# Attention decode: the last head's output is written from its 128x4 tile by one DMA of 2-byte elements

## The chip, the core and the metric

The kernel runs on one core of a Trainium2 chip. The metric is the device time of one execution in microseconds (us). Before the change the median of three runs is 628.26 us (628.16 to 628.30).

## What is computed

One decode step of grouped-query attention. There are 32 query heads with one query each, and 8 key/value heads of 65,536 positions, each of 128 numbers in bf16. Four query heads share one key/value head.

```python
B, Hq, Hkv, Sq, Sk, D = 1, 32, 8, 1, 65536, 128

def reference(q, k, v):
    rep = Hq // Hkv                       # 4 query heads to a key/value head
    k = jnp.repeat(k, rep, axis=1)
    v = jnp.repeat(v, rep, axis=1)
    scale = D ** -0.5
    scores = jnp.einsum("bhqd,bhkd->bhqk", q, k) * scale
    p = softmax(scores, axis=-1)
    return jnp.einsum("bhqk,bhkd->bhqd", p, v)
```

The result is 32 rows of 128 bf16 numbers, 8 KB in all, one row after the other in DRAM. The keys and values read for it are 268 MB.

## The kernel before

Each key/value head is cut into four units of 16,384 positions, and two units make a pair: 16 pairs in all. For a unit TensorE transposes 128 blocks of 128 keys (`pe_transposes`, L135), VectorE and ScalarE copy the transposed blocks out of PSUM (`evict`, L207 and L205), TensorE multiplies them by the four queries of the head (`pe_scores`, L144), VectorE and GpSimd find the maximum, ScalarE takes the exponentials (`exps`), and TensorE sums the values weighted by them (`pe_values`, L162) into a PSUM tile `pvb` of 128 numbers by 4 queries. A running maximum and a running sum (`acc`, `lp`) join the units of a head.

Each engine has a queue of its own, written out by hand in `tensor_engine`, `vector_engine`, `scalar_engine`, `gpsimd_engine` and `sync_engine`, and waits on semaphores. SyncE (SP) issues all loads of keys and values in the order of use, and after them the stores.

The division by the softmax sum leaves a head's output in four columns of the SBUF tile `oT`, 128 numbers (partitions) by 4 queries: L310 for the heads before the last, L305 for the last one. In DRAM the 128 numbers of a query lie in a row, so the tile has to be turned round on its way there. The two cases differ:

- **Heads 0 to 6.** The columns are shifted along as heads come in, and in the last head's first half VectorE transposes all of `oT` in 32x32 blocks into `orow` (L282). SP writes `orow` by four DMAs of 28 rows of 64 bytes (L445), which are issued right behind the last loads.
- **Head 7, the last.** L305 writes the last four columns of `oT` and raises the semaphore `t_f`. TensorE, which waits for `t_f`, transposes the 128x4 columns into a PSUM tile `trb` of 4x128 (L191) and raises `s_x`. VectorE, which waits for `s_x`, copies this to the SBUF tile `lrow` of 4x128 (L339) and raises `t_row`. SP, which waits for `t_row`, writes `lrow` by one DMA of four rows of 256 bytes (L448), with the semaphore `l_sem`.

At the end of the block the engines meet at a barrier (the instructions at L450), and SP waits until all stores have landed: at L457 for `o_sem` (the four DMAs) and then for `l_sem`.

The semaphore `t_f` is raised once per head and never lowered, so that its value is 8 once the last head's output stands in `oT`.

Of the kernel before, what the change touches and what calls it, by code (L numbers as in the profile page):

```python
# [5 lines left out]
DT = mybir.dt  # L6
# [4 lines left out]
P = 128  # L11
# [30 lines left out]
def starts(sizes):  # L42
    return [sum(sizes[:i]) for i in range(len(sizes))]
# [8 lines left out]
def bass_standalone__gqa_softmax__decode_kernel(nc, q, k, v, out):  # L52
    _, Hq, _, D = q.shape
    _, H, Sk, _ = k.shape
    R = Hq // H
    HR = H * R
# [4 lines left out]
    kf, vf, qf, of = k[0], v[0], q[0, :, 0, :], out[0, :, 0, :]  # L61
# [4 lines left out]
    def sb(name, shape, dt):  # L66
        return S(nc.sbuf_tensor(name, shape, dt))

    def sem(name):
        return S(nc.semaphore(name))  # L70
# [10 lines left out]
    ident = sb("ident", [P, P], DT.bfloat16)  # L81
# [15 lines left out]
    oT = sb("oT", [P, HR], DT.bfloat16)  # L97
    otmp = sb("otmp", [P, HR], DT.bfloat16)
    orow = sb("orow", [P, HR], DT.bfloat16)
    lrow = sb("lrow", [R, D], DT.bfloat16)  # L100
    dscr = sb("dscr", [P, 2], DT.float32)

    trb = [S(nc.psum_tensor(f"trb{i}", [P, TB * P], DT.bfloat16)) for i in range(NTB)]
# [12 lines left out]
    cm, cma, ng, dmr, exd, sx, lrd, lra = (sem(n) for n in ("cm", "cma", "ng", "dmr", "exd", "sx", "lrd", "lra"))  # L116
    acr, l_sem, lws = sem("acr"), sem("l_sem"), sem("lws")
    xd, xa, xg = sem("xd"), sem("xa"), sem("xg")
    q_sem, o_sem, s_x, t_if, t_id, t_o, t_f, t_row = (
        sem(n) for n in ("q_sem", "o_sem", "s_x", "t_if", "t_id", "t_o", "t_f", "t_row"))  # L120

    def own(e, ins, s):
        ins.then_inc(s, 1)
        take(e, s)
# [43 lines left out]
    def pe_pair(pe, lap):  # L168
        pend = []
        for n in range(2):  # L170
            for j in range(G):
                pe_transposes(pe, n, j)
                pend.append((n, j))
                if len(pend) > LAG:
                    pe_scores(pe, *pend.pop(0))
        while pend:
            pe_scores(pe, *pend.pop(0))
        for n in range(2):
            pe_values(pe, n, lap)

    def tensor_engine(pe):
        pe.wait_ge(t_id, 1)
        for _ in range(PE_LEAD):
            pe.matmul(pvb[0][0:R, 0:R], lhsT=ident[:, 0:R], rhs=ident[:, 0:R], start=True, stop=True)
        pe.wait_ge(q_sem, 16)
        pe.transpose(qps[:, 0:HR], qsb[:, :], ident[0:HR, 0:HR]).then_inc(s_x, 1)
        pe.wait_ge(t_if, 1)
        with pe.Fori(0, NP) as lap:
            pe_pair(pe, lap)
        pe.wait_ge(t_f, H)  # L190
        pe.transpose(trb[0][0:R, 0:P], oT[:, HR - R:HR], ident[:, :]).then_inc(s_x, 1)  # L191


    def evict(e, n, j):
# [24 lines left out]
    def next_queries(e):  # L219
        e.tensor_copy(qcur[:, :], qT[:, 0:R]).then_inc(qrdy, 1)  # L220
        own(e, e.tensor_copy(qtmp[:, 0:HR - R], qT[:, R:HR]), xd)
        own(e, e.tensor_copy(qT[:, 0:HR - R], qtmp[:, 0:HR - R]), xd)
# [39 lines left out]
    def dve_pair(e, second, lap):  # L262

        fresh, last = not second, second
        for j in range(G):
            if not on_act(j):
                evict(e, 0, j)
            if j == 0:
                e.sem_inc(pgo, 1)
        for j in (0, 1, 2):  # L270
            evict(e, 1, j)
        take(e, qkd)
        chunk_max(e, 0)
        evict(e, 1, 4)
        new_max(e, 0, fresh)
        for j in (5, 6, 8, 9, 10):
            evict(e, 1, j)
        rescale(e, 0, fresh)
        if fresh:
            own(e, e.tensor_copy(otmp[:, 0:HR - R], oT[:, R:HR]), xd)  # L280
            own(e, e.tensor_copy(oT[:, 0:HR - R], otmp[:, 0:HR - R]), xd)
            e.transpose(orow[:, :], oT[:, :]).then_inc(t_o, 1)  # L282
        for j in (12, 13, 14):
            evict(e, 1, j)
        take(e, qkd)
        chunk_max(e, 1)
        new_max(e, 1, False)
        if last:
            next_queries(e)
        else:  # L290
            e.sem_inc(qrdy, 1)
        values_done(e, 0, fresh)
        rescale(e, 1, False)
        if not last:
            e.wait_ge(pvd, 1)
            e.sem_inc(vfree, 1)
            values_done(e, 1, False)
            return
        e.sem_inc(acr, 1)
        e.sem_inc(lrd, 1)  # L300
        take(e, lra)
        own(e, e.reciprocal(recip[:, :], la[:, :]), xd)
        with e.If(lap == H - 1):
            e.wait_ge(pvd, 1)
            e.tensor_tensor(oT[:, HR - R:HR], pvb[1][:, 0:R], recip[:, :], ALU.mult).then_inc(t_f, 1)  # L305
        with e.Else():
            e.wait_ge(pvd, 1)
            e.sem_inc(vfree, 1)
            own(e, e.tensor_tensor(acc[:, :], acc[:, :], pvb[1][:, 0:R], ALU.add), xd)
            e.tensor_tensor(oT[:, HR - R:HR], acc[:, :], recip[:, :], ALU.mult).then_inc(t_f, 1)  # L310
        e.sem_inc(pvd, -1)

    def make_identity(e):

        e.memset(ident[:, :], 0.0)
        for i in range(3):
            e.memset(ramp[:, i:i + 1], float(i))
        own(e, e.memset(ramp[:, 3:4], 3.0), xd)
        w = 4
        while w < Q:  # L320
            own(e, e.tensor_scalar(ramp[:, w:2 * w], ramp[:, 0:w], float(w), None, ALU.add), xd)
            w *= 2
        own(e, e.transpose(rampT[:, :], ramp[:, :]), xd)
        for b in range(0, P, Q):
            ins = e.tensor_tensor(ident[b:b + Q, b:b + Q], ramp[b:b + Q, :], rampT[b:b + Q, :], ALU.is_equal)
        ins.then_inc(t_id, 1)

    def vector_engine(e):
        make_identity(e)
        e.memset(oT[:, :], 0.0)  # L330
        e.memset(dm[:, :], 0.0)
        e.wait_ge(s_x, 1)
        own(e, e.tensor_copy(qT[:, :], qps[:, 0:HR]), xd)
        next_queries(e)
        with e.Fori(0, H) as lap:
            dve_pair(e, False, lap)
            dve_pair(e, True, lap)
        e.wait_ge(s_x, 2)
        e.tensor_copy(lrow[:, :], trb[0][0:R, 0:P]).then_inc(t_row, 1)  # L339


    def exps(e, n):
# [55 lines left out]
    def sync_engine(e):  # L398
        W = T * D

        def src(x, p):
            h, c = p // 2, p % 2
            return x[h, c * 2 * P * T:(c + 1) * 2 * P * T, :].rearrange("(p t) d -> p (t d)", p=P)

        def pieces(to, s, sizes, sems):
            for a, w, sm in zip(starts(sizes), sizes, sems):
                e.dma_start(to[:, a * D:(a + w) * D], s[:, a * D:(a + w) * D]).then_inc(sm, 16)

        def tokens(sems):
            for sm in sems:  # L410
                e.sem_inc(sm, 16)

        for p in range(NP):
            ks, vs = src(kf, p), src(vf, p)
            if p:
                e.wait_ge(kfree, 3 * p)
            if WHOLE[0] <= p < WHOLE[1]:
                e.dma_start(kbuf[:, :], ks).then_inc(kp[0][0], 16)
                tokens(kp[0][1:])
            else:  # L420
                for n in range(2):
                    if n and p:
                        e.wait_ge(bfree, p)
                    to, s = bbuf if n else kbuf, ks[:, n * W:(n + 1) * W]
                    if p == 0 or (p == NP - 1 and n == 0):
                        pieces(to, s, K_PIECES[n], kp[n])
                    else:
                        e.dma_start(to[:, 0:W], s).then_inc(kp[n][0], 16)
                        tokens(kp[n][1:])
                e.sem_inc(cpg, len(POOL_COPIES))  # L430
                e.sem_inc(cpa, len(sum(ACT_COPIES.values(), ())))
            if p:
                e.wait_ge(vfree, p)
            if WHOLE[0] <= p < WHOLE[1]:
                tokens(kp[1])
            if p < NP - 1:
                e.dma_start(vbuf[:, :], vs).then_inc(vp[0][0], 16)
                tokens(vp[1])
            else:
                for n in range(2):  # L440
                    pieces(vbuf[:, n * W:(n + 1) * W], vs[:, n * W:(n + 1) * W], V_PIECES[n], vp[n])
        e.wait_ge(t_o, H)
        for b, rows in enumerate(OUT_ROWS):
            for r, n in zip(starts(rows), rows):
                e.dma_start(of[r:r + n, b * Q:(b + 1) * Q],  # L445
                            orow[b * Q + r:b * Q + r + n, :]).then_inc(o_sem, 16)
        e.wait_ge(t_row, 1)
        e.dma_start(of[HR - R:HR, :], lrow[:, :]).then_inc(l_sem, 16)  # L448

    with nc.Block() as block:  # L450
        block.tensor(tensor_engine)
# [34 lines left out]
```

## Time and profile before

The profile is one execution, taken by the hardware profiler.

| What | us |
|---|---|
| Median of three runs | 628.26 |
| Span of the profiled execution, first to last instruction | 626.94 |
| What the median has beyond the span | 1.32 |
| Last weighted sum of values ends, L305 starts | 625.00 |
| TensorE's transpose L191 starts | 625.22 |
| VectorE's copy L339 starts | 625.52 |
| SP issues the last DMA, L448 | 625.77 |
| SP's last wait, L457, is over | 626.9 |

The profiled execution's own device time is not listed apart from its span; the 1.32 us are the median less the span.

How to read the rows. PE is TensorE, PEld its weight loads, DVE VectorE, ACT ScalarE, POOL GpSimd, SP SyncE; a q behind the name (SPq) marks instructions of an engine's sequencer, among them the issue of a DMA. L305 is line 305 of the program. A row of the timeline has the start, the duration in us, the engine, the line, the operation, output and input tile, their shapes, the number of instructions, and in brackets how long the engine had been idle and what ended that. A row on waits reads: who waited, for whom, us in total, times, longest. A view of DMA in a window divides the window into 40 slices: first the busy share of the 16 DMA engines in tenths, then the rate in GB/s, then the number of packets. A packet is one contiguous piece that one DMA engine moves, or the 4 bytes by which it raises a semaphore.

### The profile page before, as it was taken

What the parts mean: (1) busy time and instruction counts of PE and PEld (TensorE: products, weight loads), DVE (VectorE), ACT (ScalarE), POOL (GpSimd) and SP (SyncE); (2) the same over time, 40 slices, a digit from 0 to 9 for tenths busy, and PEclk for the clock granted to TensorE, in tenths of its full rate; (3) what the DMA queues carried; (4) which work ended last, traced back from release to release, by engine and by line L of the source; (5) the groups of instructions that cost most, each with busy time, mean ns of one, the idle gap of its engine ahead of it and who ended that gap; (6) DMA issues with size and microseconds to landing.
All of it is one profiled execution on the core that took longest, in us unless ns stands there. A gap on an engine that the chain in (4) does not pass through costs nothing. (4 is left out here: it accounts for less than half of the span.)

```text
span 626.9 us, 27931 instructions
## 1 busy us (share of the span) xinstructions
PE 484.6 (77%) x12340; PEld 478.9 (76%) x12340; DVE 315.1 (50%) x699; ACT 228.9 (37%) x445; POOL 159.9 (26%) x124
## 2 busy tenths in 40 slices
PE   5752995959859498694976959679496894999698
PEld 5752995949859498694976959679496894999698
DVE  4620752817537174371734717356183562848274
ACT  2320532615335153341634407245062441624133
POOL 0000704307042070520605115060150702400000
PEclk9965875958769587695966959678596785969597
DMA  8999999999999999999999999999999999999997
GB/s 366 440 449 424 439 431 439 431 439 426 443 422 447 410 460 410 460 406 460 410 439 431 426 443 426 443 426 439 431 439 431 439 431 435 416 447 424 420 433 302
DMA packets 6280, 268.57 MB, mean 428 GB/s; under 512 B 896, under 2 KB 1024, under 8 KB 1152
## 3 DMA queue, kind: packets, MB, share of 16 engines
q1 hardware_dynamic: 6224, 268.45, 99.2%
q8 instruction: 6, 0.10, 0.1%
q10 hardware_dynamic: 48, 0.01, 0.0%
q14 instruction: 2, 0.02, 0.0%
HBM read 268.44 MB, written 0.01 MB: 428 GB/s over the span
## 5 line engine op out<-in xcount | busy, mean ns | idle before, releaser
L207 DVE COPY ktb<-trb 128x1024 bf16<-128x1024 bf16 x384 | 254.6, 689 | 177.5 <-PE trb L135 173.7
L205 ACT ACTIVATE ktb<-trb 128x1024 bf16<-128x1024 bf16 x128 | 131.0, 1023 | 352.7 <-PE trb L135 297.9
L135 PE MATMUL trb<-ident,kbuf 128*128 128x128 bf16 x2048 | 177.1, 245 | 104.7 <-PEq L49 104.6
L135 PEld LDWEIGHTS trb<-ident,kbuf 128*128 128x128 bf16 x2048 | 143.9, 111 | 105.6 <-issue 105.5
L213 POOL COPY bbuf<-kbuf 128x2048 bf16<-128x2048 bf16 x78 | 143.9, 1893 | 177.6 <-POOLq L49 177.6
L144 PE MATMUL qkb<-qcur,ktb 128*128 128x4 bf16 x4096 | 174.3, 165 | 11.8 <-PEq L49 10.3
L144 PEld LDWEIGHTS qkb<-qcur,ktb 128*128 128x128 bf16 x4096 | 155.2, 97 | 14.6 <-issue 14.6
L135 PE MATMUL trb<-ident,bbuf 128*128 128x128 bf16 x2048 | 157.0, 220 | 5.2 <-issue 3.9
L162 PE MATMUL pvb<-pts,vbuf 128*128 128x4 bf16 x4096 | 113.0, 166 | 15.2 <-PEq L49 11.0
L162 PEld LDWEIGHTS pvb<-pts,vbuf 128*128 128x128 bf16 x4096 | 111.1, 103 | 16.6 <-issue 15.6
L135 PEld LDWEIGHTS trb<-ident,bbuf 128*128 128x128 bf16 x2048 | 117.4, 97 | 5.5 <-issue 5.5
L393 POOL PARTITION_ALL_REDUCE cmaxa<-cmax x32 | 11.9, 370 | 254.1 <-POOLq L49 254.1
L347 ACT ACTIVATE pts<-qkb,negm 128x128 bf16<-128x128 f32 x128 | 50.9, 549 | 37.2 <-ACTq L49 37.2
L356 ACT ACTIVATE bbuf<-kbuf 128x2048 bf16<-128x2048 bf16 x26 | 49.5, 1902 | 0.0
L347 ACT ACTIVATION_READ_ACCUMULATOR pts<-qkb,negm 128x1 f32 x128 | 35.6, 278 | 0.0
L225 DVE TENSOR_REDUCE cmax<-qkb 128x4 f32<-128x512 f32 x32 | 22.0, 686 | 23.4 <-DVEq L49 23.4
L259 DVE TENSOR_TENSOR acc<-acc,pvb 128x4 f32<-128x4 f32 x16 | 2.5, 158 | 30.0 <-PE pvb L162 30.0
L257 DVE COPY acc<-pvb 128x4 f32<-128x4 f32 x8 | 1.3, 163 | 21.8 <-PE pvb L162 21.8
L395 POOL PARTITION_ALL_REDUCE la<-lp x8 | 3.4, 430 | 30.7 <-POOLq L49 30.7
L236 DVE SCALAR_TENSOR_TENSOR negm<-cmaxa,m 128x4 f32<-128x4 f32 x24 | 3.9, 163 | 11.7 <-DVEq L49 11.5
L351 ACT ACTIVATE alpha<-dm 128x4 f32<-128x4 f32 x32 | 7.1, 221 | 0.0
L250 DVE TENSOR_TENSOR acc<-acc,alpha 128x4 f32<-128x4 f32 x24 | 3.9, 164 | 6.1 <-DVEq L49 5.7
(44 smaller groups left out, 41.6 us busy)
## 6 DMA issues: line engine op xcount, KB each, us to landing
kbuf<-in_k_dram SPq DMA_DIRECT2D x4, 2048.0 KB, 16.3
bbuf<-in_k_dram SPq DMA_DIRECT2D x2, 4096.0 KB, 20.9
bbuf<-in_k_dram SPq DMA_DIRECT2D x2, 2048.0 KB, 19.9
kbuf<-in_k_dram SPq DMA_DIRECT2D x1, 4096.0 KB, 16.3
vbuf<-in_v_dram SPq DMA_DIRECT2D x1, 4096.0 KB, 21.9
vbuf<-in_v_dram SPq DMA_DIRECT2D x1, 2336.0 KB, 27.1
vbuf<-in_v_dram SPq DMA_DIRECT2D x1, 1216.0 KB, 29.6
vbuf<-in_v_dram SPq DMA_DIRECT2D x1, 416.0 KB, 30.1
```

Of the source, the lines that this page charges most:

```text
L135: ins = pe.transpose(trb[j % NTB][:, i * P:(i + 1) * P], kv[:, t, :], ident[:, :])
L144: ins = pe.matmul(qkb[n][:, t * R:(t + 1) * R], lhsT=ktb[:, off:off + P], rhs=qcur[:, :], start=True, stop=True)
L162: ins = pe.matmul(pvb[n][:, 0:R], lhsT=vv[:, t, :], rhs=pts[n][:, t * R:(t + 1) * R], start=t == 0, stop=t == T - 1)
L205: e.activation(dst, trb[j % NTB][:, :], AF.Copy).then_inc(eva, 1)
L207: e.tensor_copy(dst, trb[j % NTB][:, :]).then_inc(evd, 1)
L213: ins = op(bbuf[:, c * CB * D:(c + 1) * CB * D], kbuf[:, off:off + CB * D])
L225: e.tensor_reduce(cmax[:, :], qkb[n][:, :].rearrange("p (t g) -> p g t", g=R), AX.X, ALU.max).then_inc(cm, 1)
L236: return e.scalar_tensor_tensor(to[:, :], cmaxa[:, :], -scale, mo[:, :], ALU.mult, ALU.min)
L347: ins = e.activation(pv[:, g, :], sv[:, g, :], AF.Exp, bias=negm[:, g:g + 1], scale=scale, accum_out=rsum[:, g:g + 1])
L351: e.activation(alpha[:, :], dm[:, :], AF.Exp, scale=1.0).then_inc(sx, 1)
L356: return e.activation(o, i, AF.Copy)
L393: e.partition_all_reduce(cmaxa[:, :], cmax[:, :], P, bass.bass_isa.ReduceOp.max).then_inc(cma, 1)
```

## The change

TensorE's transpose L191, VectorE's copy L339, the tile `lrow` and the semaphore `t_row` are gone. SP waits for `t_f` in place of `t_row` and issues one DMA whose source is the last four columns of `oT` as they stand. Its destination is the same 4x128 piece of the output, walked along the 128 numbers first and the 4 queries inside, so that each element of 2 bytes is a piece by itself.

```diff
@@ tensor_engine
         with pe.Fori(0, NP) as lap:
             pe_pair(pe, lap)
-        pe.wait_ge(t_f, H)
-        pe.transpose(trb[0][0:R, 0:P], oT[:, HR - R:HR], ident[:, :]).then_inc(s_x, 1)
@@ vector_engine
         with e.Fori(0, H) as lap:
             dve_pair(e, False, lap)
             dve_pair(e, True, lap)
-        e.wait_ge(s_x, 2)
-        e.tensor_copy(lrow[:, :], trb[0][0:R, 0:P]).then_inc(t_row, 1)
@@ sync_engine
-        e.wait_ge(t_row, 1)
-        e.dma_start(of[HR - R:HR, :], lrow[:, :]).then_inc(l_sem, 16)
+        e.wait_ge(t_f, H)
+        with nc.allow_non_contiguous_dma(reason="the last head's output is written as it stands, d by g"):
+            e.dma_start(of[HR - R:HR, :].rearrange("g d -> d g"), oT[:, HR - R:HR]).then_inc(l_sem, 16)
```

SP's queue at the end of the program, before. A row has the line, the kind, output and input, the shape in elements, and the semaphore that it waits for:

```order
L407 DMA vbuf<-in_v_dram 128x512
L445 DMA out_dram<-orow 28x32 [waits t_o]
L445 DMA out_dram<-orow 28x32 x3
L448 DMA out_dram<-lrow 4x128 [waits t_row]
L450 UNCONDITIONAL_BRANCH
```

And with the change:

```order
L402 DMA vbuf<-in_v_dram 128x512
L440 DMA out_dram<-orow 28x32 [waits t_o]
L440 DMA out_dram<-orow 28x32 x3
L444 DMA out_dram<-oT 128x4x1 [waits t_f]
L446 UNCONDITIONAL_BRANCH
```

The last DMA stays where it was in the queue; its wait and its shape are others. The line numbers of the changed program are smaller by five here.

VectorE's queue at its end, before:

```order
L305 TENSOR_TENSOR oT<-pvb,recip 128x4 [waits pvd]
L303 UNCONDITIONAL_BRANCH
L309 TENSOR_TENSOR acc<-acc,pvb 128x4 [waits pvd]
L310 TENSOR_TENSOR oT<-acc,recip 128x4 [waits xd]
L306 UNCONDITIONAL_BRANCH
L335 REGISTER_ALU
L335 COMPARE_AND_BRANCH
L339 COPY lrow<-trb 4x128 [waits s_x]
L450 UNCONDITIONAL_BRANCH
```

And with the change:

```order
L302 TENSOR_TENSOR oT<-pvb,recip 128x4 [waits pvd]
L300 UNCONDITIONAL_BRANCH
L306 TENSOR_TENSOR acc<-acc,pvb 128x4 [waits pvd]
L307 TENSOR_TENSOR oT<-acc,recip 128x4 [waits xd]
L303 UNCONDITIONAL_BRANCH
L332 REGISTER_ALU
L332 COMPARE_AND_BRANCH
L446 UNCONDITIONAL_BRANCH
```

Nothing else of VectorE's queue moved; the multiplication by the reciprocal is now the last thing that it computes.

More of the change, by code (lines that the diff above doesn't have):

```diff
@@ L99, in bass_standalone__gqa_softmax__decode_kernel @@
     orow = sb("orow", [P, HR], DT.bfloat16)
-    lrow = sb("lrow", [R, D], DT.bfloat16)
     dscr = sb("dscr", [P, 2], DT.float32)
@@ L118, in bass_standalone__gqa_softmax__decode_kernel @@
     xd, xa, xg = sem("xd"), sem("xa"), sem("xg")
-    q_sem, o_sem, s_x, t_if, t_id, t_o, t_f, t_row = (
-        sem(n) for n in ("q_sem", "o_sem", "s_x", "t_if", "t_id", "t_o", "t_f", "t_row"))
+    q_sem, o_sem, s_x, t_if, t_id, t_o, t_f = (
+        sem(n) for n in ("q_sem", "o_sem", "s_x", "t_if", "t_id", "t_o", "t_f"))
     def own(e, ins, s):
```

## The prediction

> **What bounds the kernel now.** I read the header and the table of DMA first, then the chain that ended last, then the timeline of the last two microseconds, and last the DMA packets of that stretch.
>
> One row of the windows, over the whole span, and two rows of the page on DMA:
>
> ```profile
> 0.00:626.94 626.94, 484.59 (x12340) 478.87 (x12340) 315.11 (x699) 228.87 (x445) 159.88 (x124) 0.78 0.99 428
> ...
> DMA  8999999999999999999999999999999999999997
> q1 hardware_dynamic: 6224, 268.45, 99.2%
> ```
>
> The DMA engines are busy for 99% of the span at 428 GB/s, so the loads set the time until the last values are there. The change touches none of them: it lies behind the last load. So the time is read from the tail, from the chain and the timeline (VectorE, TensorE and SP apart):
>
> ```profile
> 623.39 1.59 PE pvb L162 x55
> 624.98 0.02 issue
> 625.00 0.17 DVE oT L305
> 625.18 0.04 issue
> 625.22 0.28 PE trb L191
> 625.50 0.02 issue
> 625.52 0.21 DVE lrow L339
> ...
> 625.00 0.16 DVE L305 TENSOR_TENSOR oT<-pvb,recip 128x4 bf16<-128x4 f32 x1 [1.78 <-PE pvb L162]
> 625.22 0.27 PE L191 MATMUL trb<-ident,oT 128*4 128x128 bf16 x1 [0.25 <-DVE oT L305]
> 625.52 0.21 DVE L339 COPY lrow<-trb 4x128 bf16<-4x128 bf16 x1 [0.36 <-PE trb L191]
> 625.77 0.25 SPq L448 DMA_DIRECT2D out_dram<-lrow  x1
> ...
> SPq L448 <- DVE lrow L339: 28.9, 1, 28.9
> SPq L457 <- DMA out_dram<-lrow: 0.4, 1, 0.4
> ...
> L457 SPq EVENT_SEMAPHORE  x1: 28/28/28, 626.9 to 626.9; - x1
> ```
>
> Nothing overlaps here: L305, then L191, then L339, then the DMA, then its landing, with 0.02 to 0.06 us between one and the next. SP has waited 28.9 us for `lrow` when it issues, and then 0.4 us for the DMA after everything else is over. Every tenth saved or added from 625.00 on shows in full in the time. From there to the end are 626.94 - 625.00 = 1.94 us; 0.2% of the time, about what a measurement can tell from no change, is 1.26 us.
>
> What the last DMA does in its 1.17 us is in the DMA view of two short windows, 626.48 to 626.60 and the 0.4 us behind it:
>
> ```profile
> GB/s 0 0 0 0 0 0 85 0 0 0 1 85 0 0 85 1 0 0 1 0 0 0 0 0 85 0 0 0 1 0 0 0 0 0 0 0 0 0 0 0
> DMA packets 8, 0.00 MB, mean 9 GB/s; under 512 B 8, under 2 KB 8, under 8 KB 8
> ...
> DMA packets 0, 0.00 MB, mean 0 GB/s; under 512 B 0, under 2 KB 0, under 8 KB 0
> ```
>
> Each slice is 0.003 us. Four slices with 85 GB/s are the four rows of 256 bytes, four with 1 GB/s are four semaphore packets, so four DMA engines move one row each. The first packet starts in slice 6, at 626.50, that is 0.73 us after the issue began; the last row starts in slice 24, at 626.55, 0.05 us later; no packet starts after 626.6, and the wait ends at 626.9. From the last packet to the end of the wait are thus 0.34 us.
>
> **What is removed.** L191, L339 and two handoffs. Now SP starts 625.77 - (625.52 + 0.21) = 0.04 us after the end of L339, and L305 ends at 625.00 + 0.16 = 625.16; with the same handoff the new DMA is issued at 625.20. That is 0.57 us earlier. TensorE then ends with its last values at 624.98 and VectorE with L305, and neither has anything queued behind it but the barrier. The wait for `t_f` on SP holds up nothing either: behind it are the barrier and L457. The semaphore itself is the one that releases L191 now, so nothing new has to be raised.
>
> **Is there something the earlier DMA would run into?** The four stores of `orow` are in the same queue, ahead of it. Their last packets stand in the window 624.10 to 624.16, and the window from 624.15 on holds only the eight packets of the last DMA:
>
> ```profile
> DMA  0040000040003000400004000030000000000000
> GB/s 0 0 43 0 0 0 0 0 43 0 0 0 3 0 0 0 43 0 0 0 0 43 0 0 0 0 3 0 0 0 0 0 0 0 0 0 0 0 0 0
> DMA packets 6, 0.00 MB, mean 4 GB/s; under 512 B 6, under 2 KB 6, under 8 KB 6
> ...
> DMA packets 8, 0.00 MB, mean 0 GB/s; under 512 B 8, under 2 KB 8, under 8 KB 8
> ```
>
> The new DMA's first packets are due at 625.20 + 0.73 = 625.93, 1.8 us after the engines fell idle. No collision is booked.
>
> **What is added.** In place of 4 rows of 256 bytes there are 128 x 4 = 512 pieces of 2 bytes. Three things can cost.
>
> The issue. Rows by number of pieces:
>
> ```profile
> L448 SPq DMA_DIRECT2D out_dram<-lrow x1: 253/253/253, 625.8 to 625.8; - x1
> L437 SPq DMA_DIRECT2D vbuf<-in_v_dram x15: 327/328/328, 2.9 to 558.3; - x15
> ```
>
> Four rows take 253 ns and 128 rows 328 ns, 0.6 ns for each row more. If the sequencer sees 128 partitions this is +0.08 us; if it sees 512 pieces, 508 x 0.6 = +0.30 us. I take 0.08, since the tile has the 128 partitions of the loads. The other end, that each piece costs 253/4 = 63 ns, would be 32 us; the 128 rows exclude it for rows, not for elements.
>
> The spread over engines. The first load starts its packets like this, in the window 1.70 to 2.30, with slices of 0.015 us:
>
> ```profile
> GB/s 0 0 2185 1092 0 1092 0 0 0 0 0 1092 0 1092 1092 1092 1092 2185 1092 0 0 0 0 0 0 0 0 0 0 1092 0 0 0 1092 0 1092 0 1092 0 0
> DMA packets 16, 0.26 MB, mean 437 GB/s; under 512 B 0, under 2 KB 0, under 8 KB 0
> ```
>
> Sixteen packets start between slice 2 and slice 37, and none of them is followed by a second: so a tile of 128 partitions goes to 16 engines, and the last starts 0.52 us after the first. With four engines it was 0.05. Bounds 0 to +0.47 us; I take 0.20, below the middle, since that load was the cold start of the program.
>
> The pieces. 512 over 16 engines are 32 on each. The lower bound of a piece is the start-to-start time of the small stores above: in the window of 0.06 us a slice is 1.5 ns, and the two 64-byte rows of a DMA on one engine start in slices 2 and 8 and in 16 and 21, 8 to 9 ns apart. 32 x 0.008 = 0.26 us. The upper bound is that each piece waits for the answer of the one before, the 0.34 us from the last packet to the end of the wait: 32 x 0.34 = 10.9 us. No row shows a store of less than 64 bytes. What separates it from the 64-byte rows: in the output, 32 neighbouring elements share 64 bytes, and they come from different partitions and so from up to eight engines at once; whatever serves a 64-byte piece has to take in 32 small writes in place of one. That speaks against the lower end, and the 64-byte rows, which do not wait for each other, speak against the upper. No row is nearer to one than to the other in what matters, the shared 64 bytes, and I take the geometric middle, sqrt(0.008 x 0.34) = 0.052 us, an estimate from these two rows: 32 x 0.052 = 1.67 us. The single row that it replaces cost 0.01.
>
> Two statements of the Trainium skill bear on this. "DMA: Bandwidth & Descriptors", section "Rules for kernel authors", says that a strided last dimension becomes one descriptor per element, which agrees with the 512 pieces; the specifications of the same page say that below 512 bytes a DMA engine reads, modifies and writes. By that rule the 64-byte and 256-byte stores would suffer as well, and the rows at 8 to 9 ns show no such wait between packets; whether 2 bytes do is what the third rival below is about, and if every piece were such a round trip the time would be that rival's 638.8 us.
>
> **The sum.** 628.26 - 0.57 + 0.08 + 0.20 + 1.67 - 0.01 = 629.63, so 629.6 us, 0.2% slower. It is made against the profiled execution (span 626.94) and carried to the median by the 1.32 us around the span, which the change does not touch.
>
> **The rivals.**
>
> *Cheap pieces: no change.* At 8 ns a piece the sum is 628.26 - 0.57 + 0.08 + 0.20 + 0.26 - 0.01 = 628.2, and without the spread 628.0. For it speaks that small packets of 64 bytes and of 4 bytes run at this pace and that SP's queue and all 16 engines are idle. Against it, the shared 64 bytes. It holds, as within 0.2%, up to a piece of (1.26 + 0.57 - 0.28 + 0.01) / 32 = 0.049 us. The time is even with the one before at 0.009 us a piece.
>
> *Faster by over 0.2%.* The removal is worth 0.57 us, and the whole tail from L305's end is 626.94 - 625.16 = 1.78. To pass 1.26 us the new DMA, with 128 times the pieces, would have to be 0.69 us shorter from issue to landing than the 1.17 us of now. Nothing in the rows speaks for that.
>
> *Each piece waits for its answer.* 628.26 - 0.57 + 0.28 + 10.88 - 0.01 = 638.8 us. For it speaks that the last wait ends 0.34 us behind the last packet, so that an answer does take that long; against it, that two 64-byte rows follow each other in 8 to 9 ns. The stretch of prices from 0.19 us a piece (634 us) upward is counted with it.
>
> *The issue is what grows.* If SP's sequencer or what stands behind it makes each of the 512 pieces, the first packets go out on time but the last wait for the maker. At the 0.6 ns this is hidden; at 10 ns a piece it is 5 us, 633 us; with cheap pieces it passes 0.2% from 1.37 / 512 = 0.003 us a piece. It would show as a long issue row or as packets of all engines evenly spaced.
>
> *The change does nothing of the kind.* The rearranged DMA could be merged into larger pieces. In the program it stands as 128x4x1, an element innermost, so I give this no chance of its own.
>
> **How the numbers follow.** Cheap pieces, 628.0 to 629.2: 0.36. The middle, 629.2 to 634, with the forecast 629.6 in it: 0.46, of which 0.06 lie below 628.26 + 1.26 = 629.52. Each piece waits, above 634: 0.10. The issue grows: 0.05. Faster: 0.03. So slower by over 0.2% is 0.40 + 0.10 + 0.05 = 0.55, within 0.2% is 0.36 + 0.06 = 0.42, faster 0.03. The range goes from 627.9, the cheap pieces without spread and with the 0.1 us by which the runs differ, to 634.0, which leaves out about 0.15 above and 0.03 below. The forecast's own case alone would be 629.2 to 634.
>
> **What would show it.** No TensorE instruction behind the last L161 and no VectorE instruction behind L302 (the new numbers of L162 and L305); the issue of the last DMA at about 0.20 us after L302 starts, lasting 0.25 to 0.55 us. In the DMA view some 512 packets of 2 bytes and 16 of 4 bytes on 16 engines, behind the last 64-byte rows. If the packets end within 0.3 us of the first one and the wait at the end still grows, the cost is in the writes and not in the issue or the engines; if they are 50 ns apart on an engine, it is in the engines; if the issue row is over 0.6 us, it is in the sequencer. The forecast is wrong if the last wait ends within 1.5 us of the issue (then pieces are cheap), or if it grows by over 6 us (then they go one by one).

## The result and the profile after

The change makes the kernel 2.15% slower: 641.67 us (median of 5, 641.07 to 642.70) against 628.26 us, ratio 1.0215, 95% interval 1.0203 to 1.0226. The forecast was 629.6 with a range from 627.9 to 634.0. The profiled execution is the fastest of the five, 641.07 us.

The tail of the changed kernel, in the timeline (VectorE, then SP), in the waits of SP, in the windows (PE, PEld, DVE, ACT and POOL busy, then clock, DMA share, GB/s) and in the DMA view from 625.9 to 626.5, in slices of 0.015 us:

```profile
624.85 0.16 DVE L302 TENSOR_TENSOR oT<-pvb,recip 128x4 bf16<-128x4 f32 x1 [1.70 <-PE pvb L161]
625.04 0.41 SPq L444 DMA_DIRECT2D out_dram<-oT  x1
...
SPq L453 <- DMA out_dram<-oT: 13.9, 1, 13.9
...
0.00:624.85 624.85, 485.76 (x12339) 480.12 (x12339) 315.07 (x698) 228.86 (x445) 159.88 (x124) 0.78 1.00 430
...
625.04:625.97 0.93, 0.00 (x0) 0.00 (x0) 0.00 (x0) 0.00 (x0) 0.00 (x0) 0.50 0.00 0
625.97:626.36 0.39, 0.00 (x0) 0.00 (x0) 0.00 (x0) 0.00 (x0) 0.00 (x0) 0.50 0.65 3
626.36:639.77 13.41, 0.00 (x0) 0.00 (x0) 0.00 (x0) 0.00 (x0) 0.00 (x0) 0.50 0.00 0
...
GB/s 0 0 0 0 0 1 2 2 3 3 4 4 4 4 4 4 3 3 3 4 3 5 4 3 3 3 2 1 1 0 0 0 0 0 0 0 0 0 0 0
DMA packets 528, 0.00 MB, mean 2 GB/s; under 512 B 528, under 2 KB 528, under 8 KB 528
```

Up to the last multiplication nothing has changed: it starts at 624.85 here and at 625.00 before. SP issues the DMA 0.19 us after it started, in place of 0.77. The issue takes 0.41 us. The 528 packets, 512 pieces and 16 for the semaphore, run from 625.97 to 626.35 and are then all gone. After that nothing works on the core for 13.41 us: no engine is busy, no DMA engine has a packet, and SP waits for the DMA to have landed. Before the change this last stretch was 0.34 us. The DMA lands, which is when its semaphore has its full value, 14.7 us after its issue:

```profile
out_dram<-oT SPq DMA_DIRECT2D x1, 1.0 KB, 14.7
```

The steps add up. From the start of the last multiplication to the end are 14.92 us in place of 1.94 (639.77 - 624.85 and 626.94 - 625.00). Of the difference, 0.58 us are won before the issue, 0.20 are lost between the issue and the first packet (0.93 us in place of 0.73) and 0.3 on the packets, and 13.07 are lost behind the last packet (13.41 in place of 0.34). So the loss is between the last packet and the landing.

### The profile page after: what moved, and what is told of

It is laid out like the page before. It is cut to its first block, busy times and chain, and to the rows that moved or that the text cites. A ratio compares the mean times of both kernels' runs of the same rounds, so it can differ in the third digit from the quotient of the medians.

```text
span 639.8 us, 27928 instructions
## 1 busy us (share of the span) xinstructions
PE 485.8 (76%) x12339; PEld 480.1 (75%) x12339; DVE 315.2 (49%) x698; ACT 228.9 (36%) x445; POOL 159.9 (25%) x124
```

## The experiments

Three theories stood against each other; with the numbers of the change they are hard to tell apart, since 32 pieces fall to each of 16 DMA engines and 32 pieces fall into each of 16 stretches of 64 bytes. E: on a DMA engine each small store waits for the one before. L: stores to the same 64 bytes go one after the other. A: all stores pass one place, at 26 ns each (13.4 us over 512 pieces).

**The removal alone.**

```diff
-            e.dma_start(of[HR - R:HR, :].rearrange("g d -> d g"), oT[:, HR - R:HR]).then_inc(l_sem, 16)
+            e.dma_start(of[HR - R:HR, :], ident[0:R, :]).then_inc(l_sem, 16)
```

> Only the removal: SP waits for t_f and writes four rows of 256 bytes, as before the change, but from the first four rows of the identity tile; the last head's output is left out (its place holds ones and zeros). All theories expect the 0.57 us of the prediction: issue of the last DMA 0.2 us after the last multiplication starts, 1.17 us from issue to the end, 627.7 us in all.

627.54 us against 628.20, ratio 0.9989 (0.9980 to 0.9998): 0.66 us faster. The timeline shows where:

```profile
624.92 0.16 DVE L302 TENSOR_TENSOR oT<-pvb,recip 128x4 bf16<-128x4 f32 x1 [1.74 <-PE pvb L161]
625.11 0.25 SPq L444 DMA_DIRECT2D out_dram<-ident  x1
```

The issue follows the multiplication after 0.19 us in place of 0.77, so 0.58 us are gained; the remaining 0.08 lie within the interval. The gain is there; the change pays it back with the store.

**Half the pieces.**

```diff
-            e.dma_start(of[HR - R:HR, :].rearrange("g d -> d g"), oT[:, HR - R:HR]).then_inc(l_sem, 16)
+            e.dma_start(of[HR - R:HR - R + 2, :].rearrange("g d -> d g"), oT[:, HR - R:HR - R + 2]).then_inc(l_sem, 16)
```

> The changed kernel with two of the last head's four queries written: 256 pieces of 2 bytes, 16 on each of 16 engines, 8 groups of 64 bytes with 32 pieces each; the other two rows are left out. Theory E (on each DMA engine a 2-byte store waits for the answer to the one before): the landing time less the fixed 1.2 us halves, from 14.7 us to about 7.9. Theory A (all stores pass one place, 26 ns each): the same 7.9. Theory L (stores to the same 64 bytes go one after another, some 0.42 us each): still 32 to a group, so still about 14.7.

641.94 us, ratio 1.0221 (1.0205 to 1.0236), the same as with all pieces:

```profile
L444 SPq DMA_DIRECT2D out_dram<-oT x1: 412/412/412, 625.1 to 625.1; - x1
...
DMA to landing us min/median/max: 15.2/15.2/15.2
```

With half the pieces on each engine and half in all, the landing takes as long. Theories E and A fall. Only L expects it: half the stretches, each with 32 pieces. The stretches are served side by side, since 8 or 16 of them take the same time.

**The distance between pieces.** Behind the end of the kernel before, a row of test stores, each waited for before the next:

```diff
...
+        with nc.allow_non_contiguous_dma(reason="measured"):
+            e.dma_start(scr[0:512].rearrange("(g d) -> d g", g=4), zsrc[:, 0:4]).then_inc(ms[0], 16)
+            e.wait_ge(ms[0], 16)
+            e.dma_start(scr[0:1024].rearrange("(d g s) -> d g s", d=128, g=4)[:, :, 0:1], zsrc[0:128, 0:4].rearrange("p (g w) -> p g w", g=4)).then_inc(ms[1], 16)
+            e.wait_ge(ms[1], 16)
...
```

> The kernel before, with a row of test stores behind its end, each waited for before the next is issued; all from a tile of zeros to a scratch tensor in DRAM, 512 pieces of 2 bytes on 16 engines. First in the pattern of the change, then with the pieces at even distances of 4, 8, 16, 32, 64, 256 and 2048 bytes, last the pattern of the change with half the pieces. Theory L: the landing time falls with the pieces that share 64 bytes, from 14.7 us to under 2.5 us at 64 bytes and beyond. Theory E and theory A: 14.7 us at every distance. The last one as in the run with half the pieces.

The stores in the pattern of the change (L459), 4 bytes apart (L461) and 256 bytes apart (L471), by their lines:

```profile
L459 SPq DMA_DIRECT2D scr<-zsrc x1: 412/412/412, 626.8 to 626.8; - x1
...
DMA to landing us min/median/max: 14.0/14.0/14.0
...
L461 SPq DMA_DIRECT2D scr<-zsrc x1: 607/607/607, 640.8 to 640.8; - x1
...
DMA to landing us min/median/max: 7.8/7.8/7.8
...
L471 SPq DMA_DIRECT2D scr<-zsrc x1: 513/513/513, 661.7 to 661.7; - x1
...
DMA to landing us min/median/max: 2.0/2.0/2.0
```

With 8, 16, 32, 64 and 2048 bytes between them it was 3.4, 3.9, 3.1, 2.8 and 2.2 us; half the pieces in the pattern of the change took 15.9 us. The same number of pieces, engines and bytes takes 14 us or 2, by where they go. Theories E and A expected 14.7 at every distance. Theory L holds in the main: the 2.8 us at 64 bytes are above the under 2.5 that it gave, and 16 bytes took longer than 8.

**The number of pieces and of engines, with pieces 1024 bytes apart.** The same kind of row of stores.

> The same kind of row of test stores, 2-byte pieces 1024 bytes apart: 128 pieces, 256, 512, 1024 and 2048 on 16 engines; then 512 pieces from 64 partitions (16 engines), from 8 partitions (8 engines) and from 4 partitions (4 engines). Theory E: 1.2 us and 0.42 us for each piece of an engine, so 4.6, 7.9, 14.7, 28 and 55 us, then 14.7, 28 and 55. Theory A: 4.6, 7.9, 14.7, 28, 55, then 14.7 three times. Theory L: all under 3 us, since no two pieces share 64 bytes.

128, 256, 512, 1024 and 2048 pieces land in 1.4, 2.0, 2.1, 3.0 and 5.3 us; 512 pieces from 64 partitions in 2.1. The 512 (L463) and the 2048 (L467):

```profile
L463 SPq DMA_DIRECT2D scr<-zsrc x1: 533/533/533, 630.4 to 630.4; - x1
...
DMA to landing us min/median/max: 2.1/2.1/2.1
...
L467 SPq DMA_DIRECT2D scr<-zsrc x1: 512/512/512, 635.5 to 635.5; - x1
...
DMA to landing us min/median/max: 5.3/5.3/5.3
...
SPq L473 <- DMA scr<-zsrc: 1.9, 1, 1.9
...
SPq L476 <- DMA scr<-zsrc: 2.7, 1, 2.7
```

The last two rows are the waits behind the stores from 8 and from 4 partitions; with the issues of 0.78 and 0.66 us these land in 2.7 and 3.4 us, with 64 and 128 pieces on an engine, where theory E expected 28 and 55. A piece of 2 bytes that lies apart from the others costs little: (5.3 - 2.1) / 96 = 0.033 us for each further piece on an engine with all 16 engines, and (3.4 - 2.7) / 64 = 0.011 from 8 engines to 4, where the number of pieces stays 512. Theory L gave under 3 us for all of these rows, and the 2048 pieces and the 4 engines are above it: it left this term out.

**The width of the stretch.** Clusters of pieces, each cluster from one engine.

```diff
...
+            e.dma_start(scr[0:1024].rearrange("(c s) -> c s", c=64)[:, 0:16:2], zsrc[:, 0:4]).then_inc(ms[0], 16)
+            e.wait_ge(ms[0], 16)
...
```

> How large is the stretch within which stores queue? Test stores behind the end of the kernel before, 512 pieces of 2 bytes each, every cluster of pieces from one DMA engine. First clusters of 8 pieces 4 bytes apart (32 bytes long), the clusters 32, 64, 128 and 512 bytes apart; then clusters of 4 pieces 4 bytes apart (16 bytes long), 16, 32, 64, 128 and 512 bytes apart. By the row of distances 16 pieces in 64 bytes land in 7.8 us, 8 in 3.4, 1 in 2.0 to 2.8. If the stretch is 64 bytes: 7.8, then 3.4 to 5 from 64 bytes on and flat; for the clusters of 4: 7.8, 3.4 to 5, then 3.0 to 3.9 and flat. If it is 32 bytes: 7.8 four times; 7.8, 3.4 to 5 and flat. If it is larger than 64 bytes, the times still fall from 64 to 128 and to 512 bytes.

> The clusters of test stores once more and in the reverse order, to tell order and chance from distance: clusters of 4 pieces (16 bytes) 512, 128, 64, 32 and 16 bytes apart, then clusters of 8 pieces (32 bytes) 512, 128, 64 and 32 bytes apart, last the pattern of the change. If the stretch is 64 bytes, as the first time: about 2.9, 2.6, 3.4 (4 to a stretch), 4.2 (8), 8.8 (16), then three times about 4 (8; the 5.0 at 512 bytes and the 2.9 at 128 were then chance), 6.9 (16) and 14 to 15. If it is larger, the cluster times fall again from 64 to 128 bytes by the same share as from 32 to 64. If the order matters, the first are slow now.

Landing in us, first run and second run:

| Clusters | every 16 bytes | 32 bytes | 64 bytes | 128 bytes | 512 bytes |
|---|---|---|---|---|---|
| 8 pieces in 32 bytes | | 6.9, 6.8 | 4.1, 3.7 | 2.9, 3.5 | 5.0, 4.5 |
| 4 pieces in 16 bytes | 8.8, 9.2 | 4.2, 4.5 | 3.4, 2.5 | 2.6, 2.8 | 2.9, 3.0 |

The clusters of 8, in the second run, at 32 (L475) and at 64 bytes (L473):

```profile
L475 SPq DMA_DIRECT2D scr<-zsrc x1: 523/523/523, 660.8 to 660.8; - x1
...
DMA to landing us min/median/max: 6.8/6.8/6.8
...
L473 SPq DMA_DIRECT2D scr<-zsrc x1: 579/579/579, 657.1 to 657.1; - x1
...
DMA to landing us min/median/max: 3.7/3.7/3.7
```

From 32 to 64 bytes the time falls in both runs and for both kinds of cluster, so the stretch is longer than 32 bytes, with nothing else changed. From 64 to 128 the clusters of 8 fall by 1.2 us in the first run and by 0.2 in the second, those of 4 fall by 0.8 and then rise by 0.3, and from there no row falls again. In the reverse order the rows come out the same within 0.9 us, and smaller differences than that between two such rows mean nothing. So 64 bytes fits best, and these rows alone do not exclude 128. The 64 clusters 512 bytes apart took longer than those 128 bytes apart in both runs (5.0 and 4.5 us against 2.9 and 3.5), where the second expectation held the first difference for chance; why is open.

**The width of the pieces, in the pattern of the change.**

> Test stores in the pattern of the change (four rows, neighbours in a row from neighbouring partitions), 512 pieces of 2, 4, 8, 16, 32 and 64 bytes, so that 32, 16, 8, 4, 2 and 1 of them share 64 bytes. If the pieces in 64 bytes count (theory L): 14, 7.8, 3.4 to 5, about 3.5, about 3 and about 2 us. If it were the number of pieces of an engine: 14 six times. Then 512 pieces of 2 bytes from 4 partitions on 4 engines, 4 bytes apart in a row, so that each 64 bytes belong to one engine: 7.8 us if stores of one engine queue for the same 64 bytes as well, 3.4 (the time of these pieces at 1024 bytes apart) if only stores of different engines get into each other's way. Then the pattern of the change once more (14), and last the same 512 pieces of 2 bytes read from DRAM into SBUF: about 2 us if it is writing that queues, 14 if reading does too.

Pieces of 2 bytes (L459), 4 bytes (L461) and 64 bytes (L469), in the pattern of the change, then the waits behind the 4 engines' pieces and behind the load:

```profile
L459 SPq DMA_DIRECT2D scr<-zsrc x1: 414/414/414, 627.0 to 627.0; - x1
...
DMA to landing us min/median/max: 14.2/14.2/14.2
...
L461 SPq DMA_DIRECT2D scr<-zsrc x1: 382/382/382, 641.2 to 641.2; - x1
...
DMA to landing us min/median/max: 9.7/9.7/9.7
...
L469 SPq DMA_DIRECT2D scr<-zsrc x1: 359/359/359, 660.5 to 660.5; - x1
...
DMA to landing us min/median/max: 1.8/1.8/1.8
...
SPq L473 <- DMA scr<-zsrc: 9.8, 1, 9.8
...
SPq L478 <- DMA zdst<-scr: 4.2, 1, 4.2
```

8, 16 and 32 bytes took 4.5, 3.3 and 1.8 us. So 512 pieces of 64 bytes, 32 times the data, land eight times as fast. The 4-byte pieces took longer than the 7.8 expected, and the 32-byte pieces, of which two share 64 bytes, no longer than those of 64 bytes, where about 3 us was expected. The pieces that share 64 bytes on a single engine queue as well: 0.78 + 9.8 = 10.6 us against 3.4 at 1024 bytes apart. Different engines are not needed for it. Reading the 2-byte pieces back took 0.36 + 4.2 = 4.6 us: far from the 14.7 of the stores in the same run, but above the 2 expected. Its packets run from 690.5 to 691.9, so the first one starts 2.9 us after the issue, and the landing follows the last one by 0.3 us: there is no long wait behind the packets as with the stores. Loads from separate 64 bytes were not run, so whether reading queues at all stays open.

"DMA: Bandwidth & Descriptors" of the Trainium skill, in its specifications, has a threshold of 512 bytes below which a DMA engine reads, modifies and writes. All the small stores here, of 2 to 256 bytes, lie below it, so no run shows whether there is a step at 512. Among them the size alone makes little difference: 512 pieces of 2 bytes far apart land in 2.0 to 2.2 us, and 512 of 64 bytes in 1.8. What makes the difference is the sharing of 64 bytes. Whether the pieces that share are read, modified and written back one after the other, no run can tell.

**Pieces of 8 bytes in the tail.**

```diff
-            e.dma_start(of[HR - R:HR, :].rearrange("g d -> d g"), oT[:, HR - R:HR]).then_inc(l_sem, 16)
+            e.dma_start(of[HR - R:HR, :].rearrange("g (d w) -> (g d) w", w=R), oT[:, HR - R:HR]).then_inc(l_sem, 16)
```

> The changed kernel with the tile's 128 rows of 8 bytes written one behind the other, so the 1024 bytes of the last head hold the right numbers in another order (d by g). 128 pieces of 8 bytes, 8 in each 64 bytes and 8 on each engine. Theory L: landing as with 8 pieces to 64 bytes, 3.4 to 5 us in place of 1.2, so 628.2 - 0.57 + 2.2 to 3.8 = 629.9 to 631.4 us. If only pieces below 4 bytes or so are slow: 627.7 us.

629.52 us, ratio 1.0018 (1.0009 to 1.0028), with a landing of 3.2 us. This is just under what theory L expected, and well above the 627.7 of the other answer: eight pieces in 64 bytes cost (3.2 - 1.4) / 8 = 0.23 us each, where 1.4 us is the landing of 128 pieces apart.

**Whole 64 bytes, turned by VectorE.**

```diff
...
-            e.tensor_tensor(oT[:, HR - R:HR], pvb[1][:, 0:R], recip[:, :], ALU.mult).then_inc(t_f, 1)
+            own(e, e.tensor_tensor(ox[:, :].rearrange("p (g s) -> p g s", g=R)[:, :, 0:1], pvb[1][:, 0:R].rearrange("p (g s) -> p g s", s=1), recip[:, :].rearrange("p (g s) -> p g s", s=1), ALU.mult), xd)
+            e.transpose(oy[:, :], ox[:, :]).then_inc(t_row, 1)
...
-        e.dma_start(of[HR - R:HR, :], lrow[:, :]).then_inc(l_sem, 16)
+        e.dma_start(of[HR - R:HR, :].rearrange("g (b c) -> b g c", c=Q),
+                    oy[0:P:Q // R, :]).then_inc(l_sem, 16)
```

> The kernel before without L191 and L339, but with whole pieces of 64 bytes: the last multiplication writes its four columns at a distance of 8 into a zeroed 128x32 tile, VectorE turns that in 32x32 blocks, and one DMA writes the 16 partitions that then hold the output, 64 bytes each, no two to the same 64 bytes. The issue comes 0.03 + 0.21 us after the multiplication in place of 0.61, some 0.33 us earlier than before; 4 pieces of an engine at 8 ns are 0.03. By theory L 627.9 us. If stores below 256 bytes were slow by themselves: no gain, 628.2 or more.

628.70 us against 628.29, ratio 1.0007 (0.9998 to 1.0016): no gain. The timeline and the wait:

```profile
624.97 0.18 DVE L304 TENSOR_TENSOR ox<-pvb,recip 128x4 bf16<-128x4 f32 x1 [1.80 <-PE pvb L163]
625.30 0.21 DVE L305 STREAM_TRANSPOSE oy<-ox 128x32 bf16<-128x32 bf16 x1
625.54 0.67 SPq L447 DMA_DIRECT2D out_dram<-oy  x1
...
SPq L457 <- DMA out_dram<-oy: 0.4, 1, 0.4
```

The issue starts 0.57 us after the multiplication in place of 0.77, so only 0.20 us are won (the transpose starts 0.15 us behind the multiplication's end, where I had put 0.03), and the issue takes 0.67 us in place of 0.25; the first packet starts at 626.84, 1.30 us after the issue began in place of 0.73. The stores themselves are quick: the wait at the end is 0.4 us as before. So the gain is lost between the start of the issue and the first packet, and not because stores below 256 bytes are slow, though that answer gave the nearer number.

**The same pieces, apart.** The last test alters only where the change's DMA writes:

```diff
-            e.dma_start(of[HR - R:HR, :].rearrange("g d -> d g"), oT[:, HR - R:HR]).then_inc(l_sem, 16)
+            e.dma_start(scr[0:128 * 4 * 512].rearrange("(g d s) -> d g s", g=4, d=128)[:, :, 0:1],
+                        oT[:, HR - R:HR].rearrange("p (g s) -> p g s", s=1)).then_inc(l_sem, 16)
```

> The changed kernel with nothing else altered than where its last DMA writes: the same 512 pieces of 2 bytes from the same tile on the same 16 engines, but 1024 bytes apart in a scratch tensor in DRAM, four rows one behind the other. The output's last four rows are left out. If what costs is that 32 pieces share 64 bytes, the landing falls from 14.7 us to the 2.0 to 2.2 us of far pieces, so 628.26 - 0.57 + 0.9 = 628.5 to 628.8 us. If it is stores of 2 bytes as such, or the DMA's 512 pieces, or 32 on an engine: 641.7 us as with the change.

628.33 us against 628.16, ratio 1.0001 (0.9992 to 1.0010), a little below the 628.5 expected:

```profile
624.93 0.41 SPq L445 DMA_DIRECT2D scr<-oT  x1
...
SPq L455 <- DMA scr<-oT: 1.1, 1, 1.1
...
DMA packets 528, 0.00 MB, mean 1 GB/s; under 512 B 528, under 2 KB 528, under 8 KB 528
...
scr<-oT SPq DMA_DIRECT2D x1, 1.0 KB, 1.9
```

The same 528 packets, the same issue of 0.41 us, and the landing takes 1.9 us in place of 14.7. So 641.67 - 628.33 = 13.3 us are the price of the elements lying side by side in DRAM, 32 to each 64 bytes, and of nothing else in the change. That they go to another tensor here does not matter: the pattern of the change into the scratch tensor took 14.0 to 14.7 us.

All landings by the number of pieces that share 64 bytes, over the rows of test stores with 512 pieces of 2 to 64 bytes on 16 engines:

| Pieces in 64 bytes | Landing, us | Less 2.0, for each piece |
|---|---|---|
| 32 | 14.0 to 14.7 | 0.38 to 0.40 |
| 16 | 6.8 to 9.7 | 0.30 to 0.48 |
| 8 | 2.9 to 5.0 | 0.11 to 0.38 |
| 4 | 2.5 to 3.9 | 0.13 to 0.48 |
| 2 | 1.8 to 3.1 | |
| 1 | 1.8 to 2.8 | |

The times rise with the pieces that share, but the price of a piece is not one number; below four the rows do not tell it from nothing.

## Why the prediction was wrong

The forecast of 629.6 was wrong by 12 us, and the range, which ended at 634.0, did not hold the time. By its steps:

- **What bounds the kernel, and the tail as the place where the change counts: right.** The loads run as before, and each tenth behind the last multiplication shows in full.
- **The removal, 0.57 us: right.** It is 0.58 in the changed kernel's timeline (0.77 to 0.19), and alone it makes the kernel 0.66 us faster, within the interval.
- **No collision with the stores of `orow`: right.** The DMA engines are idle from the multiplication to the new packets. These start at 625.97, forecast 625.93, but that closeness is luck: the multiplication itself ran 0.15 us earlier than in the profile before. Counted from its start they come after 1.12 us, forecast 0.93; the longer issue is 0.16 of that.
- **The issue, +0.08 with a bound of 0.30: a little low.** It took 0.41 us in place of 0.25, +0.16.
- **The spread and the packets, 0.20 + 0.26 us: right.** All 528 packets lie within 0.38 us. The pieces do run over the DMA engines at the pace of whole 64-byte rows, which was the lower bound: an engine is busy for 0.65 of the 0.39 us on average, with 33 packets, so 7.7 ns for each.
- **The price of a piece, 0.052 us: this is the term that failed.** It stands for the stores behind the packets, and it was (14.7 - 1.9) / 32 = 0.40 us, so 12.8 us in place of 1.67 with the packets. The step named the cause that the runs bear out, that "32 neighbouring elements share 64 bytes" and that "whatever serves a 64-byte piece has to take in 32 small writes in place of one", and then did not price it: it took the geometric middle of two rows. The pipelined 64-byte rows were used to speak against the upper bound, but each of those rows has 64 bytes to itself. They show how fast packets leave, and nothing on how fast stores to one place are served. A row of about the right size was there, the 0.34 us from the last packet to the end of the wait: if stores to one place follow each other at that pace, the sum is the 638.8 us that stood among the rivals. That the 0.40 is the same thing as that 0.34, no run shows.
- **The rival "each piece waits for its answer" at 638.8 us, chance 0.10: nearest in time, and its price nearly right (0.34 for 0.40), but its mechanism was another.** It let the pieces of an engine wait for each other. With 16 pieces on an engine in place of 32 the landing stayed at 15.2 us, and with 128 on an engine but apart it was 3.4. That 32 is both the pieces of an engine and the pieces of a stretch brought the number close.
- **The rival "cheap pieces" at 628.2 us: what the change would cost without the sharing.** The run with the pieces apart gave 628.33 beside 628.16, no difference, as that sum has it.
- **The rivals on the issue and on faster: no.** The issue row is 0.41 us, not over 0.6, and nothing was won. The signs named at the end of the prediction nearly told the cases apart: the packets ended 0.38 us after the first one, where the sign said 0.3, they were not 50 ns apart, and the wait at the end still grew, so the cost is in the writes. It grew by 13.5 us (13.9 for 0.4), over the 6 that were named as the sign of a wrong forecast.
- **Slower was forecast, with a chance of 0.55, and slower it is.** The size was not: 0.2% for 2.15%.

What stays open: what it is that serves stores to one 64 bytes one after the other, the memory or something on the way to it, which no run here separates; whether the stretch is 64 bytes or somewhat longer, which also sets how many pieces share one; why the price in the tail falls to about 0.23 us with 8 pieces of 8 bytes; and why 64 clusters 512 bytes apart take longer than 128 bytes apart.

## What to carry to other kernels

When a DMA writes elements smaller than 64 bytes, count how many of its pieces fall into the same 64 bytes of DRAM: here each of 32 cost 0.40 us, one after the other, while 512 pieces that shared nothing landed in 2 us. This cost shows in no packet and no busy row, only in the wait between the last packet and the landing, so a short store at the end of a kernel should be turned on the chip and written in whole 64 bytes or more. And when two bounds lie a factor of 40 apart (0.008 and 0.34 us), ask which of the two rows shows the thing that is disputed, before taking a middle.

## What the runs showed of the hardware that was not expected

- Stores to the same 64 bytes queue, also when they come from one DMA engine (10.6 us against 3.4), and several stretches are served side by side (8 or 16 stretches take 15.2 and 14.7 us).
- The time of an issue did not go by the count of pieces: 0.36 to 0.42 us where both sides are walked as 128x4, 0.51 to 0.61 for 512 pieces at one even distance, 0.65 for 256 pieces and 0.51 for 2048, and 0.67 us for only 16 pieces from 16 partitions that go to a 4x4 pattern. The rows go together with the shape of the two sides; why is open.
